# Linear attention and a gated feed-forward on one core: another hand-written order for the first two spans and the head of the third

## The chip, the cores and the metric

The kernel runs on one core of one Trainium2 chip. The metric is the device time of one execution in microseconds (us). TensorE (PE) does the matmuls, VectorE (DVE) and ScalarE (ACT) the elementwise work, GpSimd (POOL) and SyncE (SP) issue DMAs. Each engine executes its own instructions strictly in the order in which the program was written.

## The reference

The inputs are q, k, v of shape [8, 8, 576, 64] in fp32, two weights of [512, 1536] and one of [1536, 512].

```python
def _attn_ref(q, k, v):
    q_s = q - np.max(q, axis=-1, keepdims=True)
    q_s = np.exp(q_s)
    q_s = q_s / (np.sum(q_s, axis=-1, keepdims=True) + 1e-09)
    k_s = k - np.max(k, axis=2, keepdims=True)
    k_s = np.exp(k_s)
    k_s = k_s / (np.sum(k_s, axis=2, keepdims=True) + 1e-09)
    kv = np.einsum('bhsd,bhse->bhde', k_s, v)
    return np.einsum('bhsd,bhde->bhse', q_s, kv)

def _moe_ref(x, w_gate, w_val, w_out):
    gate = 1.0 / (1.0 + np.exp(-(x @ w_gate)))
    val = x @ w_val
    return gate * val @ w_out

x = attn_out.transpose(0, 2, 1, 3).reshape(4608, 512)
```

The attention is linear: a softmax of q along a row, one of k along the sequence, kv = kᵀv per batch and head, then q·kv. Its result x, 4608 tokens by 512, goes through the gated feed-forward. Nearly all of the arithmetic is in the three large products with the weights.

## The kernel before, in words

**Tiling.** The 4608 tokens are cut into nine spans of T = 512. For each span the attention part makes x (512 tokens by 512), and the feed-forward is made in six steps, each over 256 of the 1536 hidden columns. All large products are made in a rounded fp32 form: every operand is split into a high and a low part (`_hi` by a copy on ACT or DVE, `_lo` by a subtraction on DVE), and three products hi·hi, hi·lo, lo·hi are summed in PSUM.

**Span 0.** The gate and value products are plain: `g1_0(j, n)` (L903) is 24 matmuls for hidden block j and gate or value n; `g2_0` (L954, for the last two blocks L962) multiplies the gated block by the output weight. Meanwhile the weights arrive (`load_w`, `load_wo`), are unpacked word by word (`w_low`, `w_sign`, `w_abs`, `w_join`, and the same for `wo`) and split (`a_hi`, `a_lo`), and DVE makes the sums of weight blocks that later spans need (`w_sum`), written to DRAM by `s_save`.

**Spans 1 to 8.** A step p is made with seven products of 12 matmuls each (all L978): `g1_a11`, `g1_a12`, `g1_a22` use split weight blocks (`a_w`), `g1_s1` to `g1_s4` use split sums of blocks (`s_sb`). Between them ACT and DVE move PSUM into `sg` (L995, L999, L1003, L1007, L1011, L1014, L1018); where a product goes on adding to a PSUM tile whose value is wanted in between, it waits on PE until the copy has read it (`a11`'s copy L995 holds `s2`, `s3`'s copy L1011 holds `a22`). `g2` (L1092, 48 matmuls) then multiplies with the output weight. During span 1 the weight sums are read back (`s_in`, L427, one 128x512 tile `i` into the slot `i` of `x`, the same four slots for every step), split (`s_hi` on ACT at L430, `s_lo` on DVE) and the split form is written to DRAM (`s_store`); the output weight goes the same way (`wo_in` L351, `wo_hi` L357, `wo_lo`, `wo_store`). From span 2 on, the split weights are only loaded (`s_load`, `wo_load`).

**The attention part of the next span** is made beside the products: `k_max` (DVE), `k_max_send` and `k_max_read` (SP: 2 KB to DRAM, then spread back over 128 partitions, L527 and L541), `k_load`, `k_sub`, `k_exp` (ACT), `k_sum` (ACT, L521, exp with a running sum), `k_mm` (PE, L609), `k_done`; for q `qn_load` (SP, L680), `qn_max` (DVE, L694), `qn_sub` (L701), `qn_exp` (ACT, L707), `qn_sum`; `qn_send` puts the rows' maxima or reciprocals into DRAM and `q_spread` (SP, L728, two DMAs per call) reads them back spread out, for `qT_sub` and `qT_mul`; `x_mm` (PE, L806) and `x_ev` make x; `c_sub`, `c_hi`, `c_lo` make its combinations for the seven products.

**Order.** Spans 2 to 8 come from a loop that writes the steps in a fixed pattern. What comes before, that is spans 0 and 1 with the preparation of span 2 and part of that of span 3, is written out by hand: a string `ORDER` of 799 words, each `name.arg.arg`, which `go` (L1349 to L1353) calls one after the other. Since every engine and every DMA queue is in order, this string sets what stands behind what on PE, DVE, ACT, POOL and SP. Some names stand for the same work on another engine: `w_sign` and `wo_sign` on ACT, `w_sign_v` and `wo_sign_v` on DVE; `s_in` and `wo_in` on the SP queue, `s_in_p` and `wo_in_p` on the POOL queue; `h_hi` on DVE, `h_hi_a` on ACT; `x_ev` and `x_ev_v`.

**The start.** k's maximum for batch 0 is made by `k_top` (DVE), `k_top_tr` (four transposes on PE, L1291) and `k_diag` (DVE, L1295 and L1298); `k_less` (PE, L1270) then subtracts it in PSUM from what `k_own` (L1263) put there. `k_exp_0`, `k_mm_00`, `k_done_00`, `qf_mul`, `tr_0` (L752), `x_0` (L830), `x_ev_0` (L835) lead to the first product `g1_0.0.0`. For span 1 the same q rows go through `qf_mul` (DVE, L744) and `tr_1` (PE, L752), in the middle of span 0's products.

Of the kernel before, what the change touches and what calls it, by code (L numbers as in the profile page):

```python
# [52 lines left out]
k0_in.0 warm.16 k0_in.2 k0_in.4 warm.2 q0_in.0.2 q0_in.2.2 k_own.0 v_load.0.3 load_w.0 k_top.1  # L53
v_load.0.1 v_load.0.4 v_load.0.0 v_load.0.2 k_own.3 load_wo.0 k_own.4 k_top.2 k1T_in.0.2
load_w.1 k_own.2 tr_new load_w.2 k_own.1 qn_load.1.3 load_wo.1 k_load.1.0 k_top.3 k_top.4
qn_max.0.0 qn_max.0.1 k_top_tr qn_max.0.2 qn_sub.0.0 qn_max.0.3 qn_sub.0.1 qn_sub.0.2 k_diag
qn_exp.0.2 k_less.4 qn_exp.0.0 k_load.1.2 qn_exp.0.1 load_w.3 kv_new qn_sub.0.3 k_less.0
k_less.3 v_load.1.1 k_less.2 qn_exp.0.3 qn_sum.0.0 k_exp_0.0 k_exp_0.3 k_less.1 k_mm_00.0
k_exp_0.4 qn_sum.0.1 k_mm_00.3 k_mm_00.4 qn_sum.0.2 k_exp_0.1 load_wo.2 qn_sum.0.3 k_exp_0.2
k_mm_00.1 w_low.0 qf_mul.0.0 k_mm_00.2 k_load.1.1 tr_0.0 qn_load.1.0 qf_mul.0.2 tr_0.2  # L60
k1T_in.2.2 w_sign_v.0 warm_tr.3 qn_load.1.2 w_abs.0.0 qT_copy.0 qf_mul.0.1 tr_0.1 qf_mul.0.3
tr_0.3 w_join.0.0 a_hi.0.0 k_done_00 w_low.1 w_abs.0.1 a_lo.0.0 w_sign_v.1 wo_low.0 qT_copy.2
qT_copy.3 qT_copy.1 x_0.0 x_0.2 w_join.0.1 w_abs.1 kv_first x_ev_0.2 x_0.3 w_join.1 x_ev_0.3
x_0.1 load_w.4 x_ev_0.1 a_hi.0.1 x_ev_0.0 a_lo.0.1 wo_sign.0 wo_abs.0 w_low.2 wo_low.1
load_w.5 g1_0.0.0 a_hi.1 qn_load.1.1 g_sig_0.0 a_lo.1 w_sign_v.2 g1_0.0.1 w_sum.0.0 wo_join.0
w_sum.0.1 g_mul_0.0 wo_sign.1 w_sum.0.2 w_abs.2 g1_0.1.0 load_wo.3 w_sum.0.3 w_join.2 wo_abs.1
wo_low.2 a_hi.2 wo_sign.2 w_low.3 k_load.1.3 qn_max.1.0 a_lo.2 load_wo.4 w_sign_v.3 w_abs.3
w_join.3 a_hi.3 g_sig_0.1 s_save.0 w_low.4 g2_0.0 qn_max.1.2 g1_0.1.1 wo_join.1 load_w.6
g1_0.2.1 a_lo.3 g_mul_0.1 g1_0.2.0 w_sign.4 g2_0.1 w_sum.1.0 g_sig_0.2 w_low.5 wo_low.3
load_wo.5 w_abs.4 k_load.1.4 w_sum.1.2 load_w.7 wo_sign.3 w_sum.1.1 k_max_1 w_sign.5 wo_abs.2  # L70
w_join.4 g1_0.3.1 g1_0.3.0 g_mul_0.2 wo_abs.3 wo_save.0 w_sum.1.3 wo_join.3 a_hi.4 v_load.1.3
w_abs.5 g_sig_0.3 s_save.1 v_load.1.4 wo_low.4 wo_join.2 v_load.1.0 a_lo.4 w_low.6 w_join.5
wo_sign_v.4 load_wo.6 a_hi.5 load_w.8 load_wo.7 g1_0.4.0 g_mul_0.3 a_lo.5 wo_abs.4 qn_sub.1.0
w_sign.6 g_sig_0.4 qn_max.1.1 k_sum.1.1 w_sum.2.0 wo_low.5 wo_save.1 qn_max.1.3 w_abs.6
k_sum.1.3 w_sum.2.2 w_sum.2.1 k_max_tr.1 w_sum.2.3 qn_exp.1.0 v_load.1.2 g1_0.4.1 qn_sub.1.2
g_mul_0.4 k_max_rows.1 kv_hi.0 s_save.2 wo_sign_v.5 g1_0.5.1 w_join.6 a_hi.6 load_w.9
qn_sub.1.1 load_wo.8 g1_0.5.0 g2_0.2 w_low.7 k_sum.1.0 kv_lo.0 w_sign_v.7 w_abs.7 wo_join.4
g_sig_0.5 w_join.7 g_mul_0.5 wo_low.6 qn_sum.1.0 k_sum.1.2 wo_sign.6 wo_abs.5 a_hi.7 w_low.8
g2_0.3 a_lo.6 k_sub.1.0 k_sub.1.1 g2_0.4 qn_exp.1.1 k_sub.1.3 wo_join.5 w_sum.3.0 k_sub.1.4
wo_save.2 qn_exp.1.2 k_exp.1.1 w_sum.3.1 wo_low.7 w_sum.3.2 qn_sub.1.3 qn_sum.1.2 qn_load.2.3  # L80
k_exp.1.0 k_exp.1.3 k_exp.1.4 g1_0.6.0 k_sub.1.2 load_w.10 a_lo.7 wo_abs.6 w_sign.8 k_exp.1.2
g1_0.6.1 w_abs.8 kT_load.2.0 g2_0.5 qn_sum.1.1 wo_sign_v.7 k_mm.1.0 g_sig_0.6 wo_abs.7
wo_join.6 w_low.9 g1_0.7.0 w_join.8 qn_exp.1.3 w_sum.3.3 k_mm.1.1 load_wo.9 g_sig_0.7
w_sign_v.9 qn_sum.1.3 k_mm.1.2 g_mul_0.6 k_mm.1.3 load_w.11 wo_join.7 k_mm.1.4 kT_load.2.1
qf_mul.1.0 a_hi.8 wo_low.8 g1_0.7.1 a_lo.8 k_done.1 w_abs.9 tr_1.0 kv_hi.1 g1_0.8.0 w_join.9
kv_lo.1 g_mul_0.7 s_save.3 wo_low.9 qf_mul.1.1 g1_0.8.1 a_hi.9 w_low.10 wo_sign.8 wo_sign.9
wo_abs.8 qT_hi.1.0 w_sign_v.10 tr_1.1 qT_lo.1.0 a_lo.9 g_sig_0.8 wo_abs.9 w_abs.10 g1_0.9.0
load_wo.10 qT_hi.1.1 x_mm.1.0 qf_mul.1.3 w_join.10 w_sum.4.0 qf_mul.1.2 w_sum.4.2 wo_join.8
w_sum.4.1 w_sum.4.3 qT_lo.1.1 x_ev.1.0 g2_0.6 a_hi.10 g_sig_0.9 g_mul_0.8 wo_low.10 g2_0.7
tr_1.2 w_low.11 wo_sign.10 w_sign_v.11 qT_hi.1.2 tr_1.3 qT_lo.1.2 k_load.2.1 x_mm.1.1  # L90
k_max.2.0 x_ev.1.1 qn_load.2.2 g1_0.9.1 k_max.2.1 x_mm.1.2 c_sub.1 w_abs.11 qT_hi.1.3
wo_abs.10 s_save.4 v_load.2.1 a_lo.10 k_load.2.2 k_sum.2.1 load_wo.11 w_join.11 kT_load.2.3
wo_save.3 wo_join.10 g_mul_0.9 x_ev.1.2 qn_load.2.0 v_load.2.0 g1_0.10.0 w_sum.5.2 k_sum.2.0
a_hi.11 qT_lo.1.3 wo_join.9 c_hi.0 c_lo.0 k_load.2.3 g1_0.10.1 x_mm.1.3 a_lo.11 w_sum.5.0
w_sum.5.1 g_sig_0.10 kT_load.2.2 wo_low.11 x_ev.1.3 wo_save.4 c_sub.2 w_sum.5.3 c_sub.4
g1_0.11.0 k_load.2.0 k_max.2.2 s_hi.5.0 g_mul_0.10 s_hi.5.3 wo_sign.11 c_hi.2 g_sig_0.11
s_lo.5.3 h_hi_0.10 s_lo.5.0 wo_abs.11 s_store.5.0 v_load.2.2 h_lo_0.10 c_sub.6 g1_0.11.1
s_hi.5.1 s_hi.5.2 s_lo.5.1 c_hi.3 v_load.2.3 s_in.0.0 wo_new.1.5 s_store.5.1 wo_in.0.0
wo_hi.5.0 wo_lo.5.0 g2_0.8 k_max.2.3 c_hi.4 s_lo.5.2 wo_join.11 c_lo.2 g2_0.9 wo_store.5.0
c_hi.5 qn_load.2.1 k_load.2.4 s_in.0.1 c_lo.4 k_max_tr.2 c_lo.3 c_lo.5 c_hi.1 c_lo.1  # L100
s_store.5.2 qT_load.2.2 k_max_rows.2 g1_a11.5 s_store.5.3 wo_hi.5.1 wo_lo.5.1 wo_store.5.1
g2_0.10 c_hi.6 g_mul_0.11 s_in.0.2 g1_s2.5 s_hi.0.1 h_hi_0.11 g1_s1.5 s_lo.0.1 h_lo_0.11
qn_max.2.0 s_hi.0.0 c_lo.6 s_store.0.1 g1_s3.5 s_hi.0.2 s_lo.0.0 s_lo.0.2 s_in.0.3 s_store.0.0
k_sub.2.1 g1_s4.5 s_hi.0.3 s_store.0.2 v_load.2.4 s_lo.0.3 g1_a12.5 g1_a22.5 s_store.0.3
g1_sig.5 g1_s3_add.5 g1_end.5 g2_0.11 s_in.1.0 h_hi.1.5 s_in.1.1 h_lo.1.5 s_in.1.2 k_sum.2.3
qn_max.2.3 qn_sub.2.0 qn_max.2.1 g1_a11.0 g1_s2.0 k_sum.2.2 qn_max.2.2 kT_load.3.1 k_sub.2.0
s_hi.1.1 g1_s1.0 s_hi.1.0 s_lo.1.1 s_lo.1.0 qn_sub.2.3 wo_new.1.0 k_exp.2.0 g1_s3.0 g1_s4.0
wo_hi.0.0 s_in.1.3 wo_lo.0.0 s_hi.1.2 s_hi.1.3 g1_a12.0 kT_load.3.0 s_store.1.1 qT_load.2.1
s_lo.1.2 qn_sub.2.2 qn_sub.2.1 qn_send.2.m q_spread.2.m.3 s_store.1.0 wo_new.1.1 wo_in_p.0.1
g1_a22.0 k_sub.2.3 k_exp.2.1 qn_exp.2.2 k_sub.2.2 g1_s3_add.0 g1_sig.0 g1_end.0 q_spread.2.m.2  # L110
wo_hi.0.1 wo_lo.0.1 s_in.2.0 s_store.1.2 s_in_p.2.2 qn_exp.2.3 wo_in.1.0 k_max.3.0 s_lo.1.3
qn_exp.2.0 h_hi_a.1.0 k_exp.2.3 s_in.2.1 s_store.1.3 wo_store.0.1 wo_store.0.0 qn_exp.2.1
h_lo.1.0 s_in.2.3 g1_a11.1 k_mm.2.0 g2.1.0 qn_sum.2.0 qn_sum.2.1 k_exp.2.2 g1_s1.1 g1_a12.1
wo_hi.1.0 k_sub.2.4 qn_sum.2.2 wo_lo.1.0 s_hi.2.0 g1_s2.1 g1_s4.1 q_spread.2.m.1 s_lo.2.0
k_exp.2.4 g1_s3.1 wo_in_p.1.1 s_hi.2.1 wo_store.1.0 s_hi.2.2 g1_s3_add.1 s_store.2.0 s_lo.2.2
s_lo.2.1 g1_a22.1 s_store.2.1 k_mm.2.1 s_hi.2.3 s_store.2.2 s_in.3.2 wo_hi.1.1 qn_sum.2.3
g1_sig.1 wo_lo.1.1 wo_in_p.2.0 wo_new.1.2 k_mm.2.2 k_mm.2.3 s_lo.2.3 s_in_p.3.0 g1_end.1
k_mm.2.4 s_in_p.3.1 qT_load.2.0 q_spread.2.m.0 h_hi_a.1.1 s_store.2.3 wo_hi.2.0 qT_sub.2.2
h_lo.1.1 k_done.2 qT_sub.2.1 g1_a11.2 qT_sub.2.0 g1_s1.2 qT_load.2.3 s_hi.3.0 s_in.3.3
wo_lo.2.0 q_spread.2.r.0 g2.1.1 qT_sub.2.3 k_max.3.1 wo_in.2.1 v_load.3.4 kv_hi.2 s_lo.3.0  # L120
g1_s2.2 g1_s4.2 s_hi.3.1 kv_lo.2 s_lo.3.1 g1_s3.2 s_hi.3.3 s_lo.3.3 g1_a12.2 s_store.3.0
wo_store.1.1 wo_hi.2.1 wo_lo.2.1 s_hi.3.2 s_lo.3.2 s_store.3.1 s_store.3.3 g1_sig.2
g1_s3_add.2 g1_a22.2 wo_new.1.3 g1_end.2 s_in_p.4.0 q_spread.2.r.3 qT_exp.2.3 qT_exp.2.2
wo_in.3.0 h_hi.1.2 s_store.3.2 h_lo.1.2 qT_exp.2.0 q_spread.2.r.2 v_load.3.1 qT_mul.2.3
g1_a11.3 g1_s1.3 wo_hi.3.0 wo_lo.3.0 s_hi.4.0 g2.1.2 wo_store.2.0 s_in_p.4.2 s_in.4.1
s_in_p.4.3 g1_s2.3 s_lo.4.0 q_spread.2.r.1 s_store.4.0 wo_store.3.0 s_hi.4.1 g1_s4.3 s_lo.4.1
wo_in.3.1 g1_s3.3 v_load.3.0 g1_a12.3 s_hi.4.2 s_store.4.1 qT_exp.2.1 v_load.3.2 s_lo.4.2
s_store.4.2 qT_mul.2.0 g1_a22.3 wo_hi.3.1 qT_mul.2.1 qT_hi.2.0 wo_lo.3.1 s_hi.4.3 qT_lo.2.0
# [1277 lines left out]
```

## Time and profile before

| what | us |
|---|---|
| median of 3 executions | 932.87 (932.18 to 936.23) |
| the profiled execution's own time | 934.83 |
| span of its profile | 933.0 |
| PE busy | 910.9 (98%) |
| DVE busy | 614.4 (66%) |
| ACT busy | 484.4 (52%) |
| POOL busy | 169.5 (18%) |
| mean granted TensorE clock | 0.992 of full speed |

The profiled execution lies 2.0 us above the median and inside the range of the three. The time outside the span is 934.83 − 933.0 = 1.8 us. Busy time is a share of the whole span; it hides that PE's idle time is not spread evenly. How the idle time lies is read from the waits and from the table by stretches of 10 us, whose rows stand below.

### The profile page before, as it was taken

What the parts mean: (1) busy time and instruction counts of PE and PEld (TensorE: products, weight loads), DVE (VectorE), ACT (ScalarE), POOL (GpSimd) and SP (SyncE); (2) the same over time, 40 slices, a digit from 0 to 9 for tenths busy, and PEclk for the clock granted to TensorE, in tenths of its full rate; (3) what the DMA queues carried; (4) which work ended last, traced back from release to release, by engine and by line L of the source; (5) the groups of instructions that cost most, each with busy time, mean ns of one, the idle gap of its engine ahead of it and who ended that gap; (6) DMA issues with size and microseconds to landing.
All of it is one profiled execution on the core that took longest, in us unless ns stands there. A gap on an engine that the chain in (4) does not pass through costs nothing.

```text
span 933.0 us, 19514 instructions
## 1 busy us (share of the span) xinstructions
PE 910.9 (98%) x7972; PEld 877.5 (94%) x7972; DVE 614.4 (66%) x998; ACT 484.4 (52%) x826; POOL 169.5 (18%) x322
## 2 busy tenths in 40 slices
...
GB/s 329 375 297 280 188 256 322 299 258 362 314 275 310 306 282 250 299 329 291 256 301 327 287 252 307 308 308 246 302 310 217 212 259 324 242 179 261 215 214 69
DMA packets 95801, 256.99 MB, mean 275 GB/s; under 512 B 15512, under 2 KB 18080, under 8 KB 93664
## 3 DMA queue, kind: packets, MB, share of 16 engines
...
## 4 chain that ended last, share of the span: by engine, by line
PE 84%; DMA 6%; DVE 4%; ACT 4%; issue 1%; SPq 1%; POOL 0%; DVEq 0%; POOLq 0%; ACTq 0%
PE gv L978 46%; PE acc L1092 26%; PE gv L903 4%; DMA x<-s 2%; PE acc L954 2%; PE gv L806 2%; PE at L609 1%; DMA ring<-qn_in 1%; DMA s<-four 1%; PE at L806 1%; DVE q_m L694 1%; DMA f_last<-wo 0%; DMA lent<-k_in 0%; DMA kmax_row<-kmax_b 0%; ACT wo_raw L262 0%
## 5 line engine op out<-in xcount | busy, mean ns | idle before, releaser
L978 PE MATMUL gv<-c_hl,s_sb 128*128 128x256 f32 x2304 | 280.9, 278 | 7.4 <-ACT sg L995 5.2
L978 PEld LDWEIGHTS gv<-c_hl,s_sb 128*128 128x128 f32 x2304 | 271.8, 189 | 8.6 <-ACT sg L995 5.8
L1092 PE MATMUL acc<-wo_hl,h 128*128 128x256 f32 x2304 | 271.1, 277 | 0.0
L1092 PEld LDWEIGHTS acc<-wo_hl,h 128*128 128x128 f32 x2304 | 266.4, 188 | 0.4
L978 PE MATMUL gv<-c_hl,a_w 128*128 128x256 f32 x1728 | 222.3, 279 | 4.0 <-ACT sg L1011 4.0
L978 PEld LDWEIGHTS gv<-c_hl,a_w 128*128 128x128 f32 x1728 | 209.3, 190 | 4.8 <-ACT sg L1011 4.4
L476 POOL DMA_DIRECT2D s_sb<-s x168 | 90.6, 539 | 282.1 <-PE gv L978 281.0
L999 DVE TENSOR_TENSOR sg<-gv,sg 128x512 f32<-128x512 f32 x48 | 33.2, 691 | 145.8 <-PE gv L978 145.6
L346 POOL DMA_DIRECT2D wo_hl<-wo x84 | 45.3, 539 | 255.3 <-PE acc L1092 255.3
L995 ACT COPY sg<-gv 128x512 f32<-128x512 f32 x48 | 28.1, 585 | 121.9 <-PE gv L978 118.9
L1011 ACT COPY sg<-gv 128x512 f32<-128x512 f32 x48 | 28.1, 586 | 95.7 <-PE gv L978 95.7
L1014 DVE TENSOR_TENSOR sg<-sg 128x512 f32<-128x512 f32 x48 | 33.2, 692 | 52.1 <-ACT sg L1011 52.1
L1067 DVE TENSOR_TENSOR h<-sg,h 128x1024 fp32r<-128x1024 f32 x48 | 58.8, 1226 | 3.4 <-ACT h L1063 1.8
L1021 ACT ACTIVATE sg<-sg 128x512 f32<-128x512 f32 x48 | 30.4, 634 | 46.9 <-DVE sg L1018 45.5
L1031 DVE TENSOR_TENSOR sg<-sg 128x512 f32<-128x512 f32 x48 | 33.2, 692 | 29.7 <-ACT sg L1021 29.6
L1007 ACT COPY sg<-gv 128x512 f32<-128x512 f32 x48 | 28.2, 587 | 39.2 <-PE gv L978 39.1
L1003 ACT COPY sg<-gv 128x512 f32<-128x512 f32 x48 | 28.1, 586 | 31.9 <-PE gv L978 31.8
L903 PE MATMUL gv<-x_hi,a_w 128*128 128x256 f32 x288 | 41.8, 286 | 1.7 <-ACT x_hi L835 1.7
L903 PEld LDWEIGHTS gv<-x_hi,a_w 128*128 128x128 f32 x288 | 37.6, 193 | 3.1 <-ACT x_hi L835 2.5
L954 PE MATMUL acc<-wo_t,h 128*128 128x512 f32 x80 | 35.3, 592 | 0.0
L1018 DVE TENSOR_TENSOR sg<-gv,sg 128x512 f32<-128x512 f32 x48 | 33.2, 691 | 2.6 <-PE gv L978 0.5
L1063 DVE CAST h<-sg 128x1024 fp32r<-128x1024 f32 x44 | 30.5, 693 | 1.3
...
## 6 DMA issues: line engine op xcount, KB each, us to landing
...
four<-q_m_row SPq DMA_DIRECT2D x56, 128.0 KB, 11.4
```

Source lines behind the costliest of these rows:

```text
L346: nc.gpsimd.dma_start(out=t.rearrange("p h e -> p (h e)"), in_=wo_dram[2 * p + i].bitcast(F32R))
L476: nc.gpsimd.dma_start(out=s_sb[:, i].rearrange("p h n e -> p (h n e)"), in_=s_dram[p][:, i * n:(i + 1) * n].bitcast(F32R),)
L903: nc.tensor.matmul(ps[:, es], lhsT=w, rhs=x[:, es], start=(at == 0 and kt == 0 and e == 0), stop=(at == 2 and kt == NK - 1 and e == 1), sk ...
L954: nc.tensor.matmul(acc[0][m], lhsT=h_0[j][:, sl], rhs=wo_f32(j), start=(j == 0), stop=False, skip_group_check=True,)
L978: nc.tensor.matmul(ps[:, n], lhsT=lh(kt), rhs=c_hl[i][:, x, kt], start=(first and n == 0 and kt == 0 and lh is wh and x == 0), stop=(last ...
L999: nc.vector.tensor_tensor(out=sg[:, 0], in0=y_z["r"], in1=sg[:, 0], op=ALU.add)
L1014: nc.vector.tensor_tensor(out=sg[:, 3], in0=sg[:, 3], in1=sg[:, 2], op=ALU.add)
L1018: nc.vector.tensor_tensor(out=sg[:, 1], in0=y_z["z"], in1=sg[:, 1], op=ALU.add)
L1031: tt(out=sg[:, 0:2, 0], in0=sg[:, 0:2, 0], in1=sg[:, 0:2, 1], op=ALU.mult)
L1063: copy(out=h_part(w, p, 0), in_=sg[:, :, 0])
L1067: nc.vector.tensor_tensor(out=lo, in0=sg[:, :, 0], in1=hi.bitcast(F32), op=ALU.subtract)
L1092: nc.tensor.matmul(acc[w][m][:, es], lhsT=h[lh][:, i, sl], rhs=o[i][:, rh, es], start=(at == 0 and i == 0 and lh == 0 and rh == 0 and e == 0),
```

## The change

Only the string `ORDER` is changed; every other line is the same in both files, and both strings have 799 words. Its last lines, before and after:

```diff
-c_sub.1 k_load.3.4 x_ev.2.2 g1_s1.4 s_load.0.0 wo_in.4.1 c_sub.2 v_load.3.3 c_sub.6
-wo_store.4.0 c_sub.4 qn_load.3.2 g1_s2.4 g1_a12.4 c_hi.0 g1_s3.4 g1_s3_add.4 k_max.3.3
-s_load.0.1 qn_load.3.3 g1_s4.4 g1_a22.4 g1_sig.4 k_load.3.2 k_max.3.2 c_hi.1 g1_end.4
-wo_hi.4.1 k_max_send.3 wo_lo.4.1 c_hi.6 g2.1.4 k_max_read.3 c_hi.2 h_hi_a.1.4 c_hi.3
...
-k_load.3.3 c_lo.6 c_lo.5 c_lo.4 k_load.3.0 qn_load.3.0 wo_store.4.1
...
+s_load.0.0 g1_end.4 c_sub.6 c_hi.4 wo_hi.4.1 wo_lo.4.1 c_hi.3 c_hi.6 c_lo.2 h_hi.1.4
+qn_load.3.1 h_lo.1.4 c_lo.3 k_max.3.3 s_load.0.2 k_max_send.3 c_hi.5 c_lo.6 k_max_read.3
+qn_load.3.2 v_load.3.3 c_lo.4 g2.1.4 k_load.3.3 s_load.0.3 v_load.3.4 v_load.3.0 v_load.3.1
+wo_load.2.0 k_load.3.2 wo_store.4.1 k_load.3.4 c_lo.5 v_load.3.2
```

Words that changed their engine: `w_sign_v` 0, 3, 7, 10, 11 and `wo_sign_v` 4, 7 become `w_sign` and `wo_sign` (DVE to ACT), `wo_sign` 1, 9 go the other way; `h_hi_a` 1.0, 1.3, 1.4 become `h_hi` (ACT to DVE); several `s_in` and `wo_in` change between the SP and the POOL queue. SP issues 381 DMAs in place of 384, POOL 315 in place of 312. ACT has 50 table loads in place of 52. The number of matmuls is the same.

Of span 0's middle: before, `qf_mul.1.0` stands behind `g_mul_0.6` and `wo_join.7` on DVE, and `tr_1.0` behind `g1_0.7.1` on PE; in the change `qf_mul.1.0` and `qf_mul.1.1` stand ahead of `g_sig_0.6`, and `tr_1.0` behind `g1_0.7.0`. At the end of span 1's fourth step two `x_mm` (L806) stand between `g1_s3.3` and `g1_a22.3` on PE, where none stood.

Three places in the engines' orders follow; a row is a run of like instructions, `xN` their number.

The first is DVE at the start, from the first maximum of q's rows (L694; L701 subtracts it, L713 sums the exps). L1295 and L1298 are `k_diag`. Before:

```order
L694 TENSOR_REDUCE q_m<-lent 128x8 x3
L701 TENSOR_TENSOR lent<-lent,q_m 128x512
L694 TENSOR_REDUCE q_m<-lent 128x8
L701 TENSOR_TENSOR lent<-lent,q_m 128x512 x2
L1295 TENSOR_REDUCE kmax_249<-acc 128x4
L1298 TENSOR_TENSOR lent<-ident,kmax_249 128x512
```

and in the change:

```order
L694 TENSOR_REDUCE q_m<-lent 128x8
L701 TENSOR_TENSOR lent<-lent,q_m 128x512
L1295 TENSOR_REDUCE kmax_207<-acc 128x4
L1298 TENSOR_TENSOR lent<-ident,kmax_207 128x512
L713 TENSOR_REDUCE q_r<-lent 128x8
L256 TENSOR_SCALAR w_raw<-w_raw 128x1024
L694 TENSOR_REDUCE q_m<-lent 128x8
```

`k_diag` stands behind two q operations in place of seven.

The second is PE where span 0's last blocks (L962) meet span 1's second step (`a11.0`, the first of the L978 rows with `a_w` behind the second L962 row). Before:

```order
L962 MATMUL acc<-wo_hl,h_r 128x256 x24
L978 MATMUL gv<-c_hl,s_sb 128x256 x48
L978 MATMUL gv<-c_hl,a_w 128x256 x24
L962 MATMUL acc<-wo_hl,h_r 128x256 x24
L978 MATMUL gv<-c_hl,a_w 128x256 x12
L978 MATMUL gv<-c_hl,s_sb 128x256 x48
```

and in the change:

```order
L962 MATMUL acc<-wo_hl,h_r 128x256 x24
L978 MATMUL gv<-c_hl,s_sb 128x256 x24
L962 MATMUL acc<-wo_hl,h_r 128x256 x24
L978 MATMUL gv<-c_hl,a_w 128x256 x36
L978 MATMUL gv<-c_hl,s_sb 128x256 x12
L978 MATMUL gv<-c_hl,a_w 128x256 x12
L978 MATMUL gv<-c_hl,s_sb 128x256 x36
```

Before, `a11.0` (12) is followed by `s2.0`, which needs `a11.0`'s copy at once. In the change `a12.5`, `a22.5` and `a11.0` (36) come behind L962, and `s1.0` (12) and `a12.0` (12), which don't need that copy, stand ahead of `s2.0`.

The third is the SP queue late in span 1, where the fifth step's weight sums are read (L427 from `s_4`; L728 are the `q_spread` DMAs). Before:

```order
L427 DMA x_109<-s_3_122 128x512
L728 DMA four<-q_r_row 64x512 x2
L351 DMA f_last<-wo_2_126 128x512
L567 DMA f_last<-v_in 64x512
L728 DMA four<-q_r_row 64x512 x2
L351 DMA f_last<-wo_3_127 128x512
L728 DMA four<-q_r_row 64x512 x2
L567 DMA v_114<-v_in 128x512
L427 DMA x_109<-s_4_123 128x512
L728 DMA four<-q_r_row 64x512 x2
```

and in the change:

```order
L686 DMA q_r_row<-q_r 128x32
L427 DMA x_109<-s_3_122 128x512
L351 DMA f_last<-wo_2_126 128x512
L427 DMA x_109<-s_3_122 128x512 x2
L351 DMA f_last<-wo_2_126 128x512
L728 DMA four<-q_r_row 64x512 x8
L427 DMA x_109<-s_4_123 128x512 x2
L680 DMA ring<-qn_in 128x512
L427 DMA x_109<-s_4_123 128x512
```

The `q_spread` DMAs stand together, three of the reads from `s_4` are on this queue in place of one, and no read of v stands between.

## Rows read from the trace of the kernel before

**Rows 1.** The page, part 1: busy time of each engine and its share.

```profile
PE 910.9 (98%) x7972; PEld 877.5 (94%) x7972; DVE 614.4 (66%) x998; ACT 484.4 (52%) x826; POOL 169.5 (18%) x322
```

**Rows 2.** PE's waits from 0 to 310 us: total, times, longest.

```profile
PE gv L978 <- ACT sg L995: 5.2, 3, 2.4
PE gv L978 <- ACT sg L1011: 4.0, 2, 3.3
...
PE acc L1270 <- DVE lent L1298: 1.7, 1, 1.7
PE gv L903 <- ACT x_hi L835: 1.7, 1, 1.7
PE gv L978 <- ACT sg L1007: 1.6, 2, 0.8
...
PE gv L978 <- DVE sg L999: 0.6, 1, 0.6
PE gv L752 <- ACT h L914: 0.6, 1, 0.6
```

**Rows 3.** Busy time by stretches of 10 us; the last row sums 0 to 320.

```profile
core 0: us, PE busy (x) PEld busy (x) DVE busy (x) ACT busy (x) POOL busy (x), PEclk, DMA share, GB/s
...
100.00:110.00 10.00, 9.43 (x68) 9.14 (x67) 9.47 (x17) 8.05 (x13) 0.00 (x0) 0.84 0.57 225
...
160.00:170.00 10.00, 7.57 (x51) 7.37 (x51) 5.71 (x9) 6.90 (x14) 0.41 (x1) 0.83 0.89 305
...
220.00:230.00 10.00, 5.86 (x47) 5.47 (x46) 3.38 (x6) 3.76 (x8) 1.48 (x3) 0.97 1.04 358
230.00:240.00 10.00, 10.00 (x72) 10.00 (x72) 8.39 (x15) 9.50 (x17) 2.81 (x6) 0.86 0.87 344
...
290.00:300.00 10.00, 7.68 (x53) 7.48 (x52) 4.93 (x10) 4.96 (x10) 1.62 (x3) 0.83 1.22 277
...
sum 320.00, PE 301.56 PEld 269.95 DVE 248.63 ACT 202.90 POOL 48.77; mean PE 9.42 PEld 8.44 DVE 7.77 ACT 6.34 POOL 1.52
```

**Rows 4.** Timeline of PE: start, length, form; in brackets the idle time before.

```profile
99.60 0.98 PE L752 MATMUL gv<-ident,ring 128*128 128x128 f32 x4 [1.94 <-issue]
...
163.46 1.80 PE L978 MATMUL gv<-c_hl,s_sb 128*128 128x256 f32 x11 [2.43 <-ACT sg L995]
...
229.02 2.39 PE L978 MATMUL gv<-c_hl,a_w 128*128 128x256 f32 x11 [3.32 <-ACT sg L1011]
...
293.06 1.90 PE L978 MATMUL gv<-c_hl,s_sb 128*128 128x256 f32 x12 [2.32 <-ACT sg L995]
```

**Rows 5.** Timeline of ACT at 160 us and at 228 us, columns as in rows 4.

```profile
160.78 1.28 ACT L521 ACT_TABLE_LOAD   x1
...
227.86 0.62 ACT L430 CAST s_sb<-x 128x512 fp32r<-128x512 f32 x1 [5.22 <-DMA x<-s]
```

**Rows 6.** Timeline of the SP queue at 213 to 218 us and at 251 to 266 us.

```profile
213.12 3.16 SPq L728 DMA_DIRECT2D four<-q_r_row  x2
...
218.28 1.31 SPq L427 DMA_DIRECT2D x<-s  x1
...
251.82 0.38 SPq L527 DMA_DIRECT2D kmax_row<-k_max  x1
263.37 0.33 SPq L541 DMA_DIRECT2D kmax_b<-kmax_row  x1
...
266.17 0.39 SPq L680 DMA_DIRECT2D ring<-qn_in  x1
```

**Rows 7.** Timeline of DVE at the start, before `tr_1.0`, and in the loop's first step.

```profile
7.85 1.85 DVE L694 TENSOR_REDUCE q_m<-lent 128x8 f32<-128x512 f32 x3
...
12.02 0.68 DVE L1295 TENSOR_REDUCE kmax<-acc 128x4 f32<-128x512 f32 x1
...
98.81 0.69 DVE L744 TENSOR_TENSOR ring<-ring,q_r 128x512 f32<-128x512 f32 x1
...
277.31 2.46 DVE L694 TENSOR_REDUCE q_m<-ring 128x8 f32<-128x512 f32 x4 [7.24 <-DMA ring<-qn_in]
```

163 lines of the change are left out of this document (82 added, 81 removed).

## The prediction

> **What bounds the kernel now.** I read the busy times first: PE is busy 98% of the span and no other engine over 66% [rows 1]. Only PE's idle time and its clock can be won, 933.0 − 910.9 = 22.1 us of idle in all. The table by stretches then says where it is: in the first 320 us PE is busy 301.56 [rows 3], so 18.4 of the 22.1 lie there, about the part that `ORDER` writes. The list of PE's waits says for whom it waited [rows 2], the timeline when [rows 4]. Five stalls are over 1.5 us. Beside idle time the reader is to see the granted clock: four stretches, each during or after a stall of 1.9 us or more, run at 0.83 to 0.86 [rows 3], partly at the lower of the two levels (1.2 in place of 2.4 GHz). Such a stretch does (1 − 0.84)·10 = 1.6 us less work; the two stalls of 1.7 us at the start are followed by no such dip. So a long stall costs itself and some 1.6 us more, and the second part is not in the list of waits.
>
> **The change, term by term.** The matmuls are the same, so the sum is over stalls and dips. All of it is against the profiled execution, 934.8 us, which lies 2.0 above the median of the runs shown.
>
> *The start.* PE waits 1.7 us for `k_diag` and 1.7 for `x_hi` [rows 2]. Before, seven q operations stand ahead of `k_diag` on DVE from 7.85, and it begins at 12.02 [rows 7], so one costs (12.02 − 7.85)/7 = 0.60 us. Five fewer stand there: up to 3.0 us earlier. PE's `k_top_tr` also moves ahead of three `k_own`, which then fill the hole instead of preceding it. q's other operations come later on DVE, but are wanted only at the transposes. The four `x_ev` pieces are copied in an order that lets the first product begin sooner. The bounds are 1.0 (the second hole and part of the first stay) and 3.4 (both go). I take 2.6, near the upper end, since 3.0 is what DVE gives.
>
> *`tr_1` in the middle of span 0.* `tr_1.0` begins at 99.60 after 1.94 us of idle [rows 4]. The view gives no releaser, but DVE's `qf_mul.1.0`, whose result it reads, runs from 98.81 to 99.50 [rows 7]; `tr_1.1` waits 0.6 more [rows 2], and the clock then is 0.84, 1.6 us [rows 3]. In the change `qf_mul` 1.0 and 1.1 stand ahead of `g_sig_0.6`, about one block earlier. 1.94 + 0.6 + 1.6 = 4.1 us. The lower bound is 2.0: DVE is busy 9.47 of 10 us there [rows 3], and what is moved back (weight words, `w_sum`, `a_lo`) can come late in its turn. Five `w_sign` and two `wo_sign` leave DVE for ACT, which has room, and two come the other way. I take 4.1.
>
> *`a11.0` in span 1.* ACT has a table load at 160.78 for `k_sum`, and only behind it the copy of `a11.0`; PE stands 2.43 us [rows 4, 5], and the clock falls to 0.83, 1.7 us [rows 3]. In the change `s1.0` and `a12.0`, which don't need the copy, stand ahead of `s2.0`. Twelve such matmuls take up to 1.90 us [rows 4], so the two products can cover more than the 2.43; but `k_sum` still stands ahead of the copy, and I leave a stall of 0.4, too short for a dip. 2.43 + 1.7 − 0.4 = 3.7 us, bounds 2 to 4.1.
>
> The load takes 1.28 us and no idle time is shown before it [rows 5]. The Trainium skill, in "ScalarE: Activation LUTs", What ACT_TABLE_LOAD costs, puts each switch at about 2.66 us, because a drain of 1.38 goes with the load. By it the stall left would be 1.8 in place of 0.4, and the forecast 1.4 us higher; the row shows no such drain, and it decides.
>
> *Five small stalls in span 1.* Behind L995 (5.2 − 2.43 − 2.32 = 0.45), L1011 (4.0 − 3.32 = 0.7), L1007 (1.6, two) and L999 (0.6) stand 3.3 us [rows 2, 4]. These sit where a split of weights waits on ACT for its read, with the copy for PE behind it. Reads further ahead remove them; other places become as tight, since the same transfers come in a shorter time. Bounds 0 and 3.3, I take 1.7.
>
> *The last weight sums, `s_in.4.1`.* SP issues it at 218.28, behind `q_spread` DMAs [rows 6]. The split on ACT that wants it starts at 227.86 after 5.22 us of waiting [rows 5]; behind it in ACT's order is `s3.3`'s copy, and PE stands 3.32 us [rows 4]. Then the clock is 0.97 and 0.86 [rows 3]: 0.3 + 1.4. In the change the spreads stand together ahead of it and are sent earlier, I put the read some 12 us ahead of its split (an estimate from the products that stand between them on PE) in place of 4.4 (218.28 to 222.64, where ACT begins to wait), and two `x_mm` stand between `s3.3` and `a22.3` and cover what is left. 3.32 + 1.7 = 5.0; bounds 0 (rival 1) to 5.0. I take 5.0, because the cover on PE holds even if the read gains nothing.
>
> *The loop's first step.* PE stands 2.32 us at 293.06 [rows 4], with a clock of 0.83, 1.7 us [rows 3]. The cause is a chain: `k_max_send.3` issues at 251.82, `k_max_read.3` can issue only when it has landed, at 263.37, behind it `qn_load.3.0` at 266.17 [rows 6], and DVE waits 7.24 us for it, to 277.31 [rows 7]. In the change `k_max_send.3` stands behind `h_lo.1.4`, `c_lo.3` and `k_max.3.3` of DVE, some 6 us later against the loop's start (an estimate from DVE's operations ahead of it), but only `qn_load.3.2`, the third of four q tiles, is behind it, and DVE wants that one 1.2 us later. One moves the stall up, the other down. Bounds: gone (4.0 us won) or 4 us worse. I take 0.
>
> Elsewhere nothing is priced: the three DMAs that go from SP to POOL and the two fewer table loads (2 × 1.28 us of ACT, in 52% busy) lie beside PE's work.
>
> **Sum:** 2.6 + 4.1 + 3.7 + 1.7 + 5.0 + 0 = 17.1 us, so 934.8 − 17.1 = 917.7, and by the median **916**. With all upper bounds 23.9 us are won: 909. With all lower ones 1 + 2 + 2 + 0 + 0 − 4 = 1: 932.
>
> **Rivals.**
> 1. *The transfers, not the order, hold span 1.* The DMA share is 1.04 in the stretch of the largest stall [rows 3], and the last read took from 218.28 to 227.86. If the queue is as full when it is issued earlier, it lands no sooner, and a tile's slot in `x` is free only when the former split has read it. Against it: the share is 0.87 and 0.89 in the stretches beside, and 0.57 at 100. Then the terms of 5.0 and 1.7 go, the gain is 10.4 and the time 922; with one more stall of that kind, 3.3 + 1.7, 927.
> 2. *The stalls only move.* DVE is busy 9.47 of 10 us at 100 us [rows 3]. If a split or a weight word that was pushed back is late by as much as `qf_mul` was, the first two terms go also, and 17.1 − 5.0 − 1.7 − 2.6 − 4.1 = 3.7 remains: 929, and down to 0 if `k_sum` holds the copy as before. That is no change, by the 0.5% (4.7 us) that a measurement of this kernel can tell.
> 3. *Slower: SP's queue stops.* SP stood from 251.82 to 263.37, 11.5 us, for one 2 KB round trip [rows 6]. In the change all eight `q_spread` DMAs of the reciprocals stand ahead of three reads of the last weight sums, behind a round trip of the same kind, and `k_max_send.3` stands ahead of everything that the loop's first step reads. The Trainium skill, in "DMA: Bandwidth & Descriptors", Anatomy of one DMA, says that a semaphore wait is served on the issuing sequencer before dispatch, so all behind it waits too; the gap in the rows agrees. If both stops reach PE whole, they cost 2 × 11.5 = 23.0 us, more than 17.1 + 4.7, and the time is 916 + 23 = 939. It decides from 21.8 us. For it: a quarter of such a wait reached PE already. Against it: a wait of 7.24 us left 2.32 on PE, so the two would leave 2 × 11.5 × 0.32 = 7 us by that ratio.
>
> **How the numbers follow.** The forecast, 909 to 922, has 0.60: six separate terms, of which four have a named cause that the order removes. Rival 1, 922 to 928, has 0.22; it is the likeliest way to miss, since the transfers are nearly full. Rival 2 has 0.10 and rival 3 0.08. The first two are faster by over 0.5% (below 928.2): 0.82; the same 0.10; slower 0.08. The range of 909 to 928 holds the first two.
>
> **What would show it.** PE's waits from 0 to 300 us should add to about 7 us in place of 18.4. The first product should begin near 26 us in place of 28.77, nothing over 1 us should stand before `tr_1.0` or `s2.0`, the granted clock should stay at 0.98 or more in every stretch up to the loop, and the loop's first product should begin some 17 us sooner. Wrong would be: new waits of L978 for ACT with a DMA `x<-s` or `f_last<-wo` as ACT's own releaser (rival 1), waits of L903 on a DVE split (rival 2), or a stall over 5 us in the loop's first step, with `ring<-qn_in` as DVE's releaser (rival 3).

## The result, and the profile after

| | median us | lowest to highest | runs |
|---|---|---|---|
| before | 932.52 | 931.27 to 936.23 | 4 |
| changed | 920.29 | 918.97 to 923.57 | 4 |

The ratio is 0.9868, with a 95% interval of 0.9829 to 0.9906: faster, by 12.2 us of the medians. The profiled execution took 920.55 us with a span of 918.8, 14.2 under the span before.

The page of the changed kernel, part 1, answers to [rows 1]:

```profile
PE 905.7 (99%) x7972; PEld 872.4 (95%) x7972; DVE 611.0 (67%) x996; ACT 491.7 (54%) x826; POOL 172.1 (19%) x325
```

PE's idle time is 918.8 − 905.7 = 13.1 us in place of 22.1. PE's waits up to 300 us in the changed kernel, which answer to [rows 2], say what is left of it:

```profile
PE gv L978 <- ACT sg L995: 6.6, 1, 6.6
PE at L1250 <- POOL lent L1216: 1.1, 1, 1.1
PE gv L903 <- ACT x_hi L835: 0.6, 1, 0.6
PE gv L978 <- ACT sg L1007: 0.3, 1, 0.3
PE gv L752 <- DVE ring L774: 0.3, 1, 0.3
PE acc L830 <- DVE f_last L623: 0.2, 1, 0.2
```

They add to 9.1 us in place of 18.4; the prediction had about 7. Twelve stalls ahead of the loop have become five short ones. One stall, in the loop, is larger than any before. The stretches of 10 us that answer to [rows 3]:

```profile
100.00:110.00 10.00, 9.63 (x54) 6.71 (x53) 9.84 (x20) 9.95 (x12) 1.07 (x2) 1.00 0.49 185
...
160.00:170.00 10.00, 9.68 (x105) 9.29 (x105) 5.58 (x11) 7.54 (x14) 1.98 (x4) 1.00 0.99 359
...
270.00:280.00 10.00, 3.39 (x21) 3.19 (x20) 7.94 (x14) 7.69 (x14) 0.54 (x1) 0.81 1.12 358
280.00:290.00 10.00, 10.00 (x133) 9.74 (x131) 4.60 (x8) 3.67 (x6) 1.62 (x3) 0.84 1.02 279
```

No dip of the granted clock is left in spans 0 and 1. In the loop the clock falls to 0.81 and 0.84, which by the prediction's way of counting is (0.19 + 0.16)·10 = 3.5 us, in place of 1.7. But PE stood still in a part of that time. The 48 products from 277.78 to 285.82 took 8.04 us, where the same products take 5.44 at a clock of 1.00 (from 296.80 on), so the dip cost 2.6. The PE timeline, as [rows 4], has the first product's second part, three of the `g2` and the stall:

```profile
28.02 1.91 PE L903 MATMUL gv<-x_hi,a_w 128*128 128x256 f32 x14 [0.56 <-ACT x_hi L835]
...
139.83 1.66 PE L978 MATMUL gv<-c_hl,a_w 128*128 128x256 f32 x12
...
232.92 5.60 PE L1092 MATMUL acc<-wo_hl,h 128*128 128x256 f32 x48
...
262.84 5.60 PE L1092 MATMUL acc<-wo_hl,h 128*128 128x256 f32 x48
...
277.78 2.93 PE L978 MATMUL gv<-c_hl,s_sb 128*128 128x256 f32 x12 [6.61 <-ACT sg L995]
...
289.90 5.71 PE L1092 MATMUL acc<-wo_hl,h 128*128 128x256 f32 x48
```

The same places of the kernel before, without the stall, which [rows 4] has:

```profile
143.83 1.66 PE L978 MATMUL gv<-c_hl,a_w 128*128 128x256 f32 x12
...
251.00 5.82 PE L1092 MATMUL acc<-wo_hl,h 128*128 128x256 f32 x48
...
282.09 5.82 PE L1092 MATMUL acc<-wo_hl,h 128*128 128x256 f32 x48
...
304.33 5.71 PE L1092 MATMUL acc<-wo_hl,h 128*128 128x256 f32 x48
```

These rows also say where the stall is. The prediction, and the expectations below, call the place the loop's first step. In both kernels two `g2` of the loop stand between the head's last one (`g2.1.4`, at 232.92) and the stall (at 247.88 and 262.84 in the changed kernel), so PE stands in the loop's third step. What it waits for goes back to reads that DVE wants in the first. From here on the steps of the loop are counted by its `g2`.

What stands behind it is read on SP, as [rows 6], on DVE, as [rows 7], and on ACT:

```profile
239.73 0.38 SPq L527 DMA_DIRECT2D kmax_row<-k_max  x1
253.00 0.33 SPq L541 DMA_DIRECT2D kmax_b<-kmax_row  x1
253.42 0.66 SPq L680 DMA_DIRECT2D ring<-qn_in  x1
...
256.97 3.40 SPq L549 DMA_DIRECT2D ring<-k_in  x2
```

```profile
262.48 1.28 DVE L694 TENSOR_REDUCE q_m<-ring 128x8 f32<-128x512 f32 x2 [9.82 <-DMA ring<-qn_in]
...
274.70 1.89 DVE L572 TENSOR_TENSOR ring<-ring,kmax_b 128x512 f32<-128x512 f32 x3 [1.49 <-DMA ring<-k_in]
```

```profile
269.20 0.63 ACT L1021 ACTIVATE sg<-sg 128x512 f32<-128x512 f32 x1 [6.99 <-DVE sg L1018]
...
277.16 0.56 ACT L995 COPY sg<-gv 128x512 f32<-128x512 f32 x1
```

SP issues `k_max_send.3` at 239.73 and can go on at 253.00, 13.3 us later. Nine reads stand behind the round trip (three before). DVE waits 9.82 us for the first of them and then again for one of k. ScalarE waits 6.99 us for DVE, makes its exps from 271.72 on, and the copy that PE wants, at 277.16, stands behind the exps.

Matmul by matmul, the last product of the head (`g2.1.4`) begins at 232.92 in place of 251.00, 18.1 us sooner. At the loop's second `g2` the lead is 19.3 us (282.09 − 262.84), behind the stall 14.4 (304.33 − 289.90), and 14.4 it stays to the end. So the head gave more than the sum of 17.1, and the loop took 4.8 back: 4.3 by the longer stall and 0.9 by the longer dip, less 0.3 that a faster pace of the matmuls gave (last section).

### The profile page after: what moved, and what is told of

It reads as the page before. It is cut to its first block, busy times and chain, and to the rows that moved or that the text cites. A ratio compares the mean times of both kernels' runs of the same rounds, so it can differ in the third digit from the quotient of the medians.

```text
span 918.8 us, 19515 instructions
## 1 busy us (share of the span) xinstructions
PE 905.7 (99%) x7972; PEld 872.4 (95%) x7972; DVE 611.0 (67%) x996; ACT 491.7 (54%) x826; POOL 172.1 (19%) x325
## 4 chain that ended last, share of the span: by engine, by line
PE 89%; DMA 5%; DVE 3%; ACT 2%; issue 1%; SPq 0%; POOL 0%; POOLq 0%; DVEq 0%; ACTq 0%
PE gv L978 48%; PE acc L1092 28%; PE gv L903 3%; PE acc L954 2%; DMA ring<-k_in 2%; PE gv L806 2%; PE at L609 2%; PE at L806 1%; DMA kmax_row<-kmax_b 1%; PE at L1250 1%; DMA x<-s 1%; DMA kmax_b<-kmax_row 1%; DVE four L381 1%; DVE ring L572 0%; DMA out<-x 0%
## 5 line engine op out<-in xcount | busy, mean ns | idle before, releaser
L978 PE MATMUL gv<-c_hl,s_sb 128*128 128x256 f32 x2304 | 279.0, 277 | 6.9 <-ACT sg L995 6.6
L978 PEld LDWEIGHTS gv<-c_hl,s_sb 128*128 128x128 f32 x2304 | 270.0, 189 | 7.6 <-ACT sg L995 6.8
L978 PE MATMUL gv<-c_hl,a_w 128*128 128x256 f32 x1728 | 220.7, 277 | 0.0
L978 PEld LDWEIGHTS gv<-c_hl,a_w 128*128 128x128 f32 x1728 | 208.0, 189 | 0.5 <-issue 0.3
L995 ACT COPY sg<-gv 128x512 f32<-128x512 f32 x48 | 28.2, 587 | 123.7 <-PE gv L978 122.7
L1011 ACT COPY sg<-gv 128x512 f32<-128x512 f32 x48 | 28.2, 587 | 97.6 <-PE gv L978 97.6
L1063 DVE CAST h<-sg 128x1024 fp32r<-128x1024 f32 x47 | 32.6, 693 | 1.3
```

The source lines that it names most:

```text
L978: nc.tensor.matmul(ps[:, n], lhsT=lh(kt), rhs=c_hl[i][:, x, kt], start=(first and n == 0 and kt == 0 and lh is wh and x == 0), stop=(last ...
L1063: copy(out=h_part(w, p, 0), in_=sg[:, :, 0])
```

## The experiments

**The start and span 0 alone.** The changed order up to the first product of span 1, then the rest as before.

```diff
-k0_in.0 warm.16 k0_in.2 k0_in.4 warm.2 q0_in.0.2 q0_in.2.2 k_own.0 v_load.0.3 load_w.0 k_top.1
...
+k0_in.0 k0_in.2 k_top.1 warm.16 k_top.2 k0_in.4 k_own.0 k_top.3 q0_in.0.2 k_top.4 qn_max.0.0
...
+c_lo.3 k_max_rows.2 s_in.0.0 c_lo.5 k_load.2.2 h_lo_0.10 g1_a11.5 wo_lo.5.1 wo_store.5.1
...
```

> The changed kernel's order through the end of span 0 (up to the first product of span 1), then the words that are left in the order of the kernel before. If the gain is the sum of independent stalls: the start (0.9 us by the two traces) and tr_1 with its dip (3 to 4 us) are won, span 1's stalls of 2.4 and 3.3 us and the loop's 2.3 us stay: 4 us off the kernel before, 927 to 930. If the stalls hang together (a stall removed early only moves the next one), under 1 us: 931 to 933.

Measured: 928.0 us, ratio 0.9937 (0.9915 to 0.9960), as the first reading has it. On PE span 1's stalls stand as they did:

```profile
220.75 2.93 PE L978 MATMUL gv<-c_hl,a_w 128*128 128x256 f32 x12 [2.94 <-ACT sg L1011]
286.18 1.65 PE L978 MATMUL gv<-c_hl,s_sb 128*128 128x256 f32 x12 [2.58 <-ACT sg L995]
```

So span 0's part is won by itself, and the rest of the gain is made behind it.

**One stall of span 1 at a time, in the kernel before.** First the read alone, on SP:

```diff
+s_in.4.1
 q_spread.2.r.3
...
-s_in.4.1
```

> The kernel before with one word moved: s_in.4.1 ahead of q_spread.2.r.3 and q_spread.2.r.2, nothing else. If the order on SP's queue makes the stall: it issues at about 211 in place of 218.3, lands by 220, ScalarE does not wait, the 3.32 us and their dip go: 4 to 5 us off, 927.5 to 929. If the transfers' rate makes it (rival 1): it lands no sooner than the other reads of that step (225 to 227), and under 1.5 us are won: 931.5 to 933.

Measured: 933.87 us, ratio 1.0015 (0.9996 to 1.0033), no change. On PE:

```profile
224.86 1.65 PE L978 MATMUL gv<-c_hl,s_sb 128*128 128x256 f32 x12 [2.22 <-ACT sg L1007]
...
291.38 2.93 PE L978 MATMUL gv<-c_hl,s_sb 128*128 128x256 f32 x12 [3.56 <-ACT sg L995]
```

The stall of 3.32 on L1011 is gone, so the read was late through its place on the queue. The time has the second reading all the same, with nothing won: 2.22 us stand now at an earlier product of the same step, and the loop's stall is 3.56 in place of 2.32 [rows 4]. The 2.22 us are the wait for another read, on ACT ahead of the copy that PE wants:

```profile
223.19 0.62 ACT L357 CAST wo_hl<-f_last 128x512 fp32r<-128x512 f32 x1 [4.30 <-DMA f_last<-wo]
```

Small differences between two profiles are to be read with care: at `s2.0`, ahead of the moved word, PE stood 3.13 us here and 2.43 in the kernel before. Then the cover for `a11.0`:

```diff
 g1_a11.0
+g1_s1.0
 g1_s2.0
...
-g1_s1.0
```

> The kernel before with one word moved: g1_s1.0 ahead of g1_s2.0 in span 1, nothing else. If the wait for a11.0's copy is what costs: one product of 1.4 us covers part of the 2.43 us, a stall of about 1.0 us is left and the dip may go: 1.4 to 3.1 us off, 929.7 to 931.6. If the products only wait later for the same engine, no change: 932 to 933.5.

Measured: 933.69 us, ratio 1.0010 (0.9994 to 1.0025), no change, as the second reading has it. `s2.0` stands 1.29 us in place of 2.43, and two later places are worse:

```profile
165.12 1.65 PE L978 MATMUL gv<-c_hl,s_sb 128*128 128x256 f32 x12 [1.29 <-ACT sg L995]
...
185.76 5.97 PE L978 MATMUL gv<-c_hl,s_sb 128*128 128x256 f32 x36 [1.97 <-ACT sg L995]
...
231.36 2.93 PE L978 MATMUL gv<-c_hl,a_w 128*128 128x256 f32 x12 [4.32 <-ACT sg L1011]
```

In these two trials in span 1, a stall taken away alone came back at another place. In the first it was a read of `wo` that had not become earlier; for the second the reason is not shown. How much of the order is needed there was not tried.

**The loop's stall: which part of SP's queue.** All of these start from the changed kernel. The q read alone:

```diff
-k_max.3.3 s_load.0.2 k_max_send.3 c_hi.5 c_lo.6 k_max_read.3 qn_load.3.2
+k_max.3.3 s_load.0.2 qn_load.3.2 k_max_send.3 c_hi.5 c_lo.6 k_max_read.3
```

> The changed kernel, with qn_load.3.2 alone moved ahead of k_max_send.3 in SP's queue. Theory A (the one q read stuck behind the 2 KB round trip makes the 6.6 us stall of the loop's first step): DVE's wait of 9.8 us for it goes and most of the stall with its clock dip (3.5 us): 7 to 10 us off the changed kernel's 920.3, so 910 to 913. Theory B (all reads behind the stopped queue make it; the reads of k land at 267 to 276 us and ScalarE's exps wait for them in front of the copy): only one of eleven reads leaves the backlog, the copy still waits, 0 to 2 us off, 918 to 920.

Measured: 918.64 us, ratio 0.9837 (0.9810 to 0.9865). PE's waits from 230 us on:

```profile
PE gv L978 <- ACT sg L995: 2.6, 1, 2.6
```

The stall, still in the third step, falls by 4.0 us in the profile, so the q read made 4.0 of the 6.6. The time falls by 1.7, as theory B has it, but the two intervals overlap, and the times of the two kernels are not told apart. Neither theory holds by itself. The send earlier:

```diff
-c_sub.4 g1_a12.4
+c_sub.4 k_max.3.3 k_max_send.3 g1_a12.4
...
-c_lo.3 k_max.3.3 s_load.0.2 k_max_send.3 c_hi.5
+c_lo.3 s_load.0.2 c_hi.5
```

> The changed kernel, with k_max.3.3 and k_max_send.3 put ahead of the span-1 step's a12 product, some 8 us earlier; nothing else moves. Theories A and B both: the round trip is over at about 243 us in place of 253, all reads behind it land some 8 to 10 us earlier, the stall of 6.6 us and its dip of 3.5 us go: 910 to 913. If instead the transfers' rate sets when the reads land (a backlog that the queue's stop only hides), under 3 us off: 917 to 920.

Measured: 917.88 us, ratio 0.9832 (0.9801 to 0.9863). The time is as the last reading has it. The stall on L995 is gone, another is there, in the first step, for a weight load:

```profile
PE gv L978 <- DMA s_sb<-s: 3.0, 1, 3.0
```

The reads ahead, the send where it was:

```diff
+qn_load.3.2 k_load.3.3 k_load.3.2 k_load.3.4
 k_max_send.3
...
-qn_load.3.2
...
-k_load.3.3
...
-k_load.3.2
...
-k_load.3.4
```

> The changed kernel, with qn_load.3.2 and the three reads of k (k_load.3.3, 3.2, 3.4) moved ahead of k_max_send.3, which itself stays where it is. Theory B: the exps find their k, only the maximum is late (back at about 260 us), DVE waits some 3 to 4 us for it in place of 9.8 and PE at most 1 us: 911 to 914. Theory A gives the same as for the q read alone. If the late maximum is itself the cause, the stall stays at 5 us or more: 918 to 921.

Measured: 918.44 us, ratio 0.9837 (0.9811 to 0.9864). The stall in the third step is gone, as theory B has it, but the time is as the last reading has it. 1.0 us stand in the first step for a weight load, and 2.1 us come up in the fifth:

```profile
PE gv L978 <- ACT sg L995: 2.1, 1, 2.1
PE gv L978 <- DMA s_sb<-s: 1.0, 1, 1.0
```

The reads of k ahead of those of v, with the q read as above; then the same with the send 3 us earlier:

```diff
+qn_load.3.2
 k_max_send.3
...
-k_max_read.3 qn_load.3.2 v_load.3.3
+k_max_read.3 k_load.3.3 k_load.3.2 k_load.3.4 v_load.3.3
...
-k_load.3.3
...
-k_load.3.2
...
-k_load.3.4
```

> The changed kernel with qn_load.3.2 ahead of k_max_send.3 and, behind k_max_read.3, the three reads of k ahead of the reads of v, which the loop wants only some 45 us later. Theory B (reads behind SP's stop, in the wrong order): the last read of k lands some 3 us earlier than the 270.6 us of the kernel with the q read alone moved, the 2.6 us that PE still stood there go to under 1, and the time is 2 to 4 us under that kernel's 918.6: 914.5 to 917. Theory C (the transfers of the loop's first three steps are the bound, so what is won in one step is lost in the next): the stall goes from the first step and a new one of 1 to 3 us comes up in the second or third, 917 to 920.

```diff
-h_hi.1.4 qn_load.3.1 h_lo.1.4 c_lo.3 k_max.3.3 s_load.0.2 qn_load.3.2 k_max_send.3
+k_max.3.3 qn_load.3.1 qn_load.3.2 k_max_send.3 h_hi.1.4 h_lo.1.4 c_lo.3 s_load.0.2
```

> The same, with k_max.3.3 also ahead of h_hi.1.4 on DVE, so that k_max_send.3 issues some 2.7 us earlier. Theory B: every read behind the stop lands 2.7 us earlier and no stall is left in the loop's first step: 913 to 916. Theory C: the reads meet the weight loads on the POOL queue earlier and a product waits for its s_sb tile, as 3.0 us did with the send 7 us earlier: 916 to 920.

Measured: 921.82 us, ratio 0.9879 (0.9851 to 0.9907), and 922.25 us, 0.9883 (0.9850 to 0.9917): nothing won, and both above every range that was expected. The first of them has 1.8 us in the third step and 4.9 in the fifth, the second 5.6 in the fifth:

```profile
PE gv L978 <- ACT sg L995: 6.7, 2, 4.9
```

```profile
PE gv L978 <- ACT sg L995: 5.6, 1, 5.6
```

Then SP's idle time ahead of the send filled with the reads:

```diff
-c_sub.4 g1_a12.4
+c_sub.4 k_max.3.3 qn_load.3.1 qn_load.3.2 k_load.3.3 k_load.3.2 k_max_send.3 g1_a12.4
...
-k_max.3.3 s_load.0.2 k_max_send.3 c_hi.5 c_lo.6 k_max_read.3 qn_load.3.2 v_load.3.3
+s_load.0.2 c_hi.5 c_lo.6
+v_load.3.0 v_load.3.1 k_load.3.4 v_load.3.3 v_load.3.4 v_load.3.2 k_max_read.3
```

> The changed kernel with SP's 15 idle us ahead of k_max_send.3 and the time of its round trip filled: two reads of q and two of k ahead of it, k_max.3.3 and the send some 7 us earlier, the last read of k and the five of v between the send and k_max_read.3. Theory C' (the head's gain was partly borrowed by reads put off into the loop; ten of them land there, up to 39 us in): pulled forward into a stretch that is not full, the first step's stall goes and none comes up in the third: 910 to 914. If the transfers are full in that stretch too, the weight loads of the loop's first step are late, with a stall of 1 to 3 us on s_sb: 915 to 918.

Measured: 920.17 us, ratio 0.9869 (0.9846 to 0.9892). That is above both ranges. The weight loads of the first step are late, more than expected:

```profile
PE gv L978 <- DMA s_sb<-s: 6.1, 1, 6.1
```

Six orders of the same transfers end at 917.9 to 922.3 us, none told apart from the changed kernel's 920.3, and in each a stall stands somewhere in the loop's first five steps. In none of the six did moving reads about that round trip do more than move the stall.

**Fewer bytes beside the round trip.** Without `s_store.4` and `wo_store.4`:

```diff
-s_store.4.0 c_lo.1 g1_s4.4 s_store.4.1 g1_s3.4 kT_load.3.3 c_sub.4 g1_a12.4 wo_store.3.1
+c_lo.1 g1_s4.4 g1_s3.4 kT_load.3.3 c_sub.4 g1_a12.4 wo_store.3.1
...
-s_store.4.3 wo_store.4.0 c_hi.2
+c_hi.2
...
-    in_=wo_dram[2 * p + i].bitcast(F32R)
+    in_=wo_dram[2 * (3 if p == 4 else p) + i].bitcast(F32R)
...
-    in_=s_dram[p][:, i * n:(i + 1) * n].bitcast(F32R),
+    in_=s_dram[3 if p == 4 else p][:, i * n:(i + 1) * n].bitcast(F32R),
```

> The changed kernel without the six 512 KB writes of span 1's last step (s_store.4 and wo_store.4, 3 MB between 215 and 253 us); the loop loads step 3's weights again where it wanted these, so its output differs. No order of any other instruction moves. Theory C (the transfers' rate holds the end of the head and the loop's first steps): the 2 KB round trip that took 13.2 us is over in 5 to 8, the reads behind it land 6 to 10 us sooner, and 6.6 us of stall with 3.5 of dip shrink to under 2: 911 to 914. Theory B (the round trip is slow by itself, the order of SP's queue alone decides): the round trip stays at 11 us or more and the time at 918 to 921.

Measured: 918.19 us, ratio 0.9845 (0.9825 to 0.9865). On SP the send and the read:

```profile
240.29 0.38 SPq L527 DMA_DIRECT2D kmax_row<-k_max  x1
250.11 0.33 SPq L541 DMA_DIRECT2D kmax_b<-kmax_row  x1
```

9.8 us in place of 13.3, between what the two theories said; the time is as theory B has it, and PE's stall is 3.8 us. With 3 MB less beside it the round trip loses 3.5 us and keeps most of its length.

**The round trip itself.** The maximum as four rows in place of 512 single numbers. `k_max.3.3` also moves ahead of `h_hi.1.4`, as in the fifth of the six orders, which won nothing:

```diff
-h_hi.1.4 qn_load.3.1 h_lo.1.4 c_lo.3 k_max.3.3 s_load.0.2 k_max_send.3 c_hi.5 c_lo.6 k_max_read.3
+k_max.3.3 h_hi.1.4 qn_load.3.1 h_lo.1.4 c_lo.3 s_load.0.2 c_hi.5 c_lo.6
...
-c_lo.4 g2.1.4 k_load.3.3
+c_lo.4 g2.1.4 k_max_tr.3 k_max_rows.3 k_load.3.3
```

> The changed kernel with the maximum of k for span 3 transposed on TensorE (k_max_tr.3, right behind g2.1.4) and written as four rows of 512 bytes from the POOL queue, in place of 512 pieces of 4 bytes from SP; k_max.3.3 stands ahead of h_hi.1.4. If the pieces make the round trip long: it takes 5 to 7 us in place of 13, the reads behind it land 6 to 8 us sooner, and the time is 912 to 916. If the backlog makes it long: 10 us or more, 918 to 921.

Measured: 912.94 us (911.55 to 913.81), ratio 0.9786 (0.9762 to 0.9810), below the changed kernel's interval. The write on POOL and the read on SP:

```profile
239.58 0.51 POOL L536 DMA_DIRECT2D kmax_row<-kmax_b  x1 [4.48 <-ACT kmax_b L534]
```

```profile
242.93 0.33 SPq L541 DMA_DIRECT2D kmax_b<-kmax_row  x1
```

3.35 us in place of 13.3, and the time is as the first reading has it. The page's part 1 of this kernel:

```profile
PE 903.9 (99%) x7973; PEld 870.4 (95%) x7973; DVE 611.1 (67%) x996; ACT 492.0 (54%) x827; POOL 171.8 (19%) x326
```

Of the span of 911.4 us, 7.5 are idle. No stall of over 1.1 us is left anywhere. It beats both kernels: 7.4 us under the changed one, 19.7 under the kernel before as run beside it (932.66).

**The same in the kernel before.**

```diff
-g1_end.4 wo_hi.4.1 k_max_send.3 wo_lo.4.1 c_hi.6 g2.1.4 k_max_read.3
+g1_end.4 wo_hi.4.1 wo_lo.4.1 c_hi.6 g2.1.4 k_max_tr.3
...
-h_lo.1.4 wo_load.2.0
+h_lo.1.4 k_max_rows.3 wo_load.2.0
```

> The kernel before with the same replacement alone: the maximum of k for span 3 transposed on TensorE behind g2.1.4 and written as four rows of 512 bytes from the POOL queue, some 6 us later than the send stood; the rest of the order as before. If the loop's stall hangs on that round trip alone: the read issues at about 261 in place of 263.4, qn_load.3.0 lands 2.4 us sooner or more, the 2.3 us of stall with the dip of 1.7 mostly go: 929 to 931. If the head's order sets the rest, the kernel stays 16 us or more above the changed kernel with this replacement (912.9). If the replacement were worth the 7 us here too, whatever the order: 925 to 927.

Measured: 929.7 us, ratio 0.9965 (0.9948 to 0.9981), as the first reading has it. The loop's stall on PE is 0.50 us in place of 2.32:

```profile
289.99 1.64 PE L978 MATMUL gv<-c_hl,s_sb 128*128 128x256 f32 x12 [0.50 <-ACT sg L995]
```

With the round trip short in both, the two orders are 929.7 − 912.9 = 16.8 us apart. That is about the worth of the head's order alone, and the sum forecast 17.1 for it.

## Why the prediction was right, and where a step failed

The forecast was 916, with 909 to 928; 920.3 was measured. The direction and the range hold, and for the head the sum comes out: 17.1 forecast, 18.1 in the profile where the head ends, 16.8 by the two kernels without the loop's stall. That it comes out so closely is in part luck: span 0 was forecast at 6.7 and gave 4.0, span 1 was forecast at 10.4 and gave 14.1. One reading of the rows was wrong without consequence: six stalls of the kernel before, not five, are over 1.5 us, and all six are in the sum. Point by point:

- *The start:* 2.6 forecast, 0.9 measured (the second product begins at 30.71 in place of 31.61). Mis-sized. `k_diag` does end 2.2 us sooner, but PE does not wait for it any more. A row of DVE's timeline and one of PE's, of the changed kernel:

```profile
10.57 0.69 DVE L1298 TENSOR_TENSOR lent<-ident,kmax 128x512 f32<-128x512 f32 x1
```

```profile
13.60 1.02 PE L1270 MATMUL gv<-lent 128*128 128x512 f32 x2
```

  PE reaches the first `k_less` at 13.60, as it did at 13.64 before, where the wait of [rows 2] ended, because its own queue is full until then. Three `k_own` stand there, which came behind `k_top_tr`, and the fillers `warm.2` and `warm_tr.3` (L1250), whose products nothing reads; from 9.57 to 13.60 the fillers take 1.2 of the 4.0 us. I had counted DVE's 3.0 us as the limit where PE's own queue was. What the start would give without the fillers there was not tried.
- *`tr_1`:* 4.1 forecast. Stall and dip are gone. The first product of span 1 begins 4.0 us sooner (139.83 in place of 143.83), 0.9 of it from the start, so 3.1. Where the other 1.0 us went was not looked for.
- *`a11.0`, the small stalls, `s_in.4.1`:* 10.4 forecast, 14.1 measured from the first product of span 1 to the last of the head. No wait is left at `s2.0` where I had left 0.4. Of the five small ones 0.3 is left. With the two large stalls and their dips these make 12.1 us; the remaining 2 us or so are in no list of waits, and the last section tells where 1.3 of them are. The Trainium skill, in "ScalarE: Activation LUTs", What ACT_TABLE_LOAD costs, has 2.66 us for a switch, by which 1.8 would have been left at `s2.0`; the load's row [rows 5] has 1.28 us, and no row shows the rest.
- *The terms as a sum of separate stalls:* borne out for span 0, not for span 1. Each of two stalls removed there by itself gave nothing, and the whole order gave all of it.
- *The dips:* Some 1.6 us were added to every stall of over 1.9 us. The rows of the kernel before bear that out for that one execution, but a dip does not come with each such stall. In the kernel before with the short round trip PE stood 2.94 us at 165.26, ahead of `s2.0`, and no dip followed:

```profile
160.00:170.00 10.00, 6.69 (x56) 6.29 (x55) 6.42 (x11) 7.34 (x15) 0.00 (x0) 1.00 0.89 316
```

  The profiled execution of the kernel before had a mean granted clock of 0.992; other executions of it had up to 0.998. So the dips that the sum takes back are partly those of one execution, which may be why the two spans differ by 14.2 us and the medians by 12.2.
- *The loop's stall:* 0 forecast, with 4 us either way. This is the step that failed. PE stands 6.61 us and loses 2.6 by the dip, where it stood 2.32 and lost 1.7; 4.8 us are lost in all, and with the short round trip 7.4 are won. Its two effects were never set against each other: by its own figures a send 6 us later and a q tile wanted 1.2 us later leave DVE 4.8 us worse off, not 0. The rows bear the 6 us out: the send stands 6.8 us behind the start of `g2.1.4` (239.73 − 232.92) where it stood 0.8 (251.82 − 251.00), and DVE goes on 3.3 us later (262.48 − 232.92 against 277.31 − 251.00). And I had weighed that only `qn_load.3.2` stands behind the round trip. Eight more reads stand there, three of them reads of k that the exps in front of PE's copy need. The q read made 4.0 of the 6.61 us, since 2.62 are left with it alone moved; with the reads of k moved too nothing is left of this stall.

Rival 1 (a read issued earlier lands no sooner) fell for the read it was told of: with nothing but its place changed, `s_in.4.1` no longer made PE stand. But a read of `wo` then held ACT for 4.30 us, which is the rival's own sign. In the changed kernel ACT's waits for such reads between 190 and 232 us add to 2.4 us and make PE stand nowhere. Rival 2 (stalls only move) is what each of the two single words did, not what the whole change does. Rival 3 named the right mechanism at one of its two places, and the sign that the prediction set for it came: a stall over 5 us behind the head, with `ring<-qn_in` as DVE's releaser. The `q_spread` stop made PE stand nowhere, and the stop at `k_max_send.3` reached PE by half: 13.3 us on SP, 6.6 on PE. The Trainium skill, in "DMA: Bandwidth & Descriptors", Anatomy of one DMA, which it writes for the GpSimd queue, has a semaphore wait served on the issuing sequencer before dispatch; SP's gap from 239.73 to 253.00 agrees with it.

Why the round trip is so long is open in part. The same 2 KB as four rows took 3.35 us; 512 numbers of 4 bytes took 13.3, and 9.8 with 3 MB fewer writes beside. The replacement changes three things: the pieces, the queue, and the traffic beside. The third is easily overlooked. POOL stands 4.48 us for ACT's copy ahead of the write, its weight loads go out behind it, and the DMA engines are far from full. The first 3.3 us from the write on, in the changed kernel and with the four rows:

```profile
239.70:243.00 3.30, 3.30 (x31) 3.30 (x30) 1.96 (x5) 1.53 (x3) 0.93 (x2) 1.00 0.98 344
```

```profile
239.60:242.90 3.30, 3.30 (x31) 3.30 (x30) 2.36 (x4) 1.17 (x2) 3.12 (x6) 1.00 0.40 79
```

The kernel with fewer writes is the nearest comparison: over its round trip 107 GB/s moved, and the 512 numbers still took 9.8 us. So by an estimate from these times some 3.5 of the 10 us saved are traffic and most of the other 6.5 the pieces or the queue, which were not told apart. The Trainium skill, in "DMA: Bandwidth & Descriptors", Specifications, wants at least 512 bytes a transfer for full rate and tells of a read-modify-write below it; the times agree with it, but do not show it.
